# Carrying four row groups of the last expert into the first two tiles of each half, and writing the right half's products between the left half's tiles

## The chip, the cores and the metric

The kernel runs on one core of a Trainium2 chip. The core has a matrix engine (PE, also called TensorE) with a weight-load path of its own (PEld), a vector engine (DVE), a scalar engine (ACT), a general engine (POOL), which here issues the input loads, and SP, which here issues the stores. Sixteen DMA engines move the data for all queues. The metric is the device time of one execution in microseconds (us). The span in the profile runs from the first to the last instruction of one profiled execution, and is a little shorter than the time of that execution.

## What is computed

Attention with keys and values averaged over blocks of 8, for 8 batches and 8 heads of 576 x 64, and then a soft mixture of experts over the 4608 tokens of 512 columns:

```python
def _moe_ref(x, phi, w1, w2):            # x: 4608 x 512, 8 experts of 4 slots, F = 1024
    logits = x @ phi
    d = np.exp(logits - logits.max(0, keepdims=True))
    d /= d.sum(0, keepdims=True) + 1e-09
    slot_input = (d.T @ x).reshape(E, S_per_e, D)
    for e in range(E):
        h = np.maximum(slot_input[e] @ w1[e], 0.0)
        slot_out[e] = h @ w2[e]
    c = np.exp(logits - logits.max(1, keepdims=True))
    c /= c.sum(1, keepdims=True) + 1e-09
    return c @ slot_out.reshape(n_slots, D)
```

The output is 4608 x 512 in float32, 9.4 MB. The change lies in the last part: `h @ w2` for the last expert, and `c @ slot_out`.

## The kernel before

The attention runs over four pairs of batches and leaves, for each token, the exponentials of its logits, transposed into `cT` (128 partitions: four copies of the 32 slots; token columns). After the last pair come the two layers of the experts.

The first layer gives `h_sb`, which `turn_hidden` transposes into `hT` (128 rows of F within a group, 8 groups `fj`, 32 slot columns). `second_layer` (line 478) multiplies, for an expert and each of its 8 row groups `fj`, the 32 columns of `hT` by 128 rows of w2. The product has 32 rows only, so group `fj` writes the strip `fj % 4` of the accumulator `so_ps` in PSUM; the four strips are four partial sums that the final product adds, because `cT` holds its 32 slots four times. I call these products narrow (32 columns of weights) and the others full (128 columns).

w2 of the first seven experts arrives whole. The last expert's w2 comes as two halves of 256 columns, left and right, each in three pieces: row groups 0 to 3, 4 to 6, and 7 (`PIECES`, line 431; loads issued by POOL on line 435). PE works on it in an order written out by hand, as ACT, DVE and SP do from line 445 on.

For each half, `side` (line 551) does the following once groups 0 to 6 are in `so_ps`:

- ACT scales `so_ps` by `recC` into `so_a` (so far without group 7).
- Tiles 0 and 1 of the tokens are "carried": `product(n, cols, True)` adds, in a PSUM bank of its own, `zT[:, n]` times group 7 of w2 (line 537) and the tile's tokens times `so_a` (line 538). `zT` holds the tokens of the two tiles times the last expert's `h` of group 7, made ahead of time: line 498 puts that part of `h_sb`, scaled, into `hz` (otherwise zeros), line 501 multiplies it by `cT`, line 503 copies it out of PSUM.
- Between the two carried tiles, `second_layer` adds group 7 to `so_ps` itself, and DVE scales the whole into `so`.
- Tiles 2 to 7 are plain products of tokens and `so` (line 540).
- Each tile's product is scaled by `recR` on its way from PSUM to SBUF (`put`, line 543), on ACT (line 513) or DVE (line 515), and `store` (line 529) sends one or two tiles from SP.

The left half is finished before the right half begins. Tiles 0 to 7 are therefore stored in eleven small stores of 128 or 256 KB. After both halves, tiles 8 to 35 are made in full width of 512 columns, put by ACT and DVE in turn, and stored in four large stores (groups of 4, 6, 10 and 8 tiles). The products share five PSUM banks (`ps_f`). `busy` (line 507) writes products that are not used, while PE would wait for w2.

Of the kernel before, what the change touches and what calls it, by code (L numbers as in the profile page):

```python
# [8 lines left out]
FP = mybir.dt.float32  # L9
BF = mybir.dt.bfloat16  # L10
AF = mybir.ActivationFunctionType
ALU = mybir.AluOpType
# [6 lines left out]
def kernel(  # L19
# [10 lines left out]
    nc = tc.nc  # L30
# [4 lines left out]
    DM = H * D  # L35
    E = moe_w1.shape[0]
    F = moe_w1.shape[2]
    NS = moe_phi.shape[1]
# [10 lines left out]
    FJ = F // 128  # L49
    XW = D + NS  # L50
    HQ = H // 2
    NG = 128 // NS
# [7 lines left out]
    TILES = [(g, r) for g, (rows, _) in enumerate(GROUPS) for r in range(rows)]  # L60

    ctx.enter_context(tc.manual_schedule(engines={ET.Pool}))
    consts = ctx.enter_context(tc.tile_pool(name="consts", bufs=1))
# [10 lines left out]
    cT = persist.tile([128, 2, B * S // 2], BF)  # L74
# [80 lines left out]
    with tc.tile_pool(name="tmp", bufs=1) as tmp:  # L155
# [8 lines left out]
        for r in range(2):  # L164
            rows = slice(r * D, (r + 1) * D)
            nc.vector.tensor_copy(out=iphi[rows, :, 0:D],
                                  in_=ident[rows, rows].rearrange("p d -> p () d").to_broadcast([D, H, D]))
        spread = tmp.tile([128, J, H, NS], BF, name="spread")
        for j in range(J):
            nc.vector.tensor_tensor(out=spread[:, j],  # L170
                                    in0=phi_f[:, j].rearrange("p s -> p () s").to_broadcast([128, H, NS]),
                                    in1=head.rearrange("p h -> p h ()").to_broadcast([128, H, NS]), op=ALU.mult)
        phi_ps = ps_m.tile([128, H, NS], FP, name="phi_ps", tag="m")
        for j in range(J):
            nc.tensor.matmul(out=phi_ps, lhsT=sel[:, j].rearrange("p r a j -> p (r a j)"), rhs=spread[:, j],  # L175
                             start=(j == 0), stop=(j == J - 1))
        nc.scalar.copy(out=iphi[:, :, D:XW], in_=phi_ps)
    nc.vector.memset(siT, 0.0)
    hz = consts.tile([128, 128], BF)
    nc.vector.memset(hz, 0.0)  # L180

    att = ExitStack()
# [177 lines left out]
    def tokens(n):  # L360

        g, r = TILES[n]
        rows, base = GROUPS[g]
        step, c0 = rows // 2, base // 2 + r // 2
        return cT[:, r % 2, c0:c0 + 127 * step + 1:step]
# [64 lines left out]
    halves = [slice(0, HC), slice(HC, DM)]  # L430
    PIECES = ((0, 4), (4, FJ - 1), (FJ - 1, FJ))
    w2_half = [xsa[:, 1, i * FJ * HC:(i + 1) * FJ * HC].rearrange("p (j c) -> p j c", c=HC) for i in range(2)]
# [13 lines left out]
    post = ctx.enter_context(tc.tile_pool(name="post", bufs=1))  # L446
    ps_o = ctx.enter_context(tc.tile_pool(name="ps_o", bufs=1, space=PSUM))
    ps_f = ctx.enter_context(tc.tile_pool(name="ps_f", bufs=5, space=PSUM))

    recC = post.tile([128, 1], FP)  # L450
    h_sb = [post.tile([128, F], BF, name=f"h_sb{i}") for i in range(E // NG)]
# [24 lines left out]
    so_ps = ps_o.tile([128, DM], FP, name="so_ps")  # L476

    def second_layer(e, j0=0, j1=FJ, half=None):
        cols = slice(0, DM) if half is None else halves[half]
        for fj in range(j0, j1):  # L480
            g = fj % NG
            nc.tensor.matmul(out=so_ps[g * NS:(g + 1) * NS, cols], lhsT=hT[:, e, fj],  # L482
                             rhs=w2_at[e, fj] if half is None else w2_half[half][:, fj],
                             start=(e == 0 and fj < NG), stop=(e == E - 1 and fj >= NG), skip_group_check=True)
# [8 lines left out]

    J7 = FJ - 1
    P7 = (E - 1) % NG * NS
    nc.vector.tensor_scalar(out=hz[P7:P7 + NS], in0=h_sb[(E - 1) // NG][P7:P7 + NS, J7:F:FJ], scalar1=recC[P7:P7 + NS],
                            scalar2=None, op0=ALU.mult)
    z_ps = ps_f.tile([128, 2, 128], FP, name="z_ps", tag="f")  # L500
    nc.tensor.matmul(out=z_ps, lhsT=hz, rhs=cT[:, :, 0:128], start=True, stop=True)
    zT = post.tile([128, 2, 128], BF)
    nc.scalar.copy(out=zT, in_=z_ps)

    idle = ps_m.tile([128, 512], FP, name="idle_ps", tag="m")

    def busy(n):
        for _ in range(n):
            nc.tensor.matmul(out=idle, lhsT=ident, rhs=cT[:, 0, 0:512], start=True, stop=True)

    def scaled(engine, dst, src, by):
        if engine == 0:
            nc.scalar.activation(out=dst, in_=src, func=AF.Copy, scale=by)  # L513
        else:
            nc.vector.tensor_scalar(out=dst, in0=src, scalar1=by, scalar2=None, op0=ALU.mult)  # L515

    so_a = post.tile([128, DM], BF)
    so = post.tile([128, DM], BF)
# [3 lines left out]
    n = 0  # L522
# [6 lines left out]
    def store(g, r0, r1, cols):  # L529
        home, dst = places[g]  # L530
        nc.sync.dma_start(out=dst[:, r0:r1, cols], in_=home[:, r0:r1, cols])

    def product(n, cols, carried=False):
        ps = ps_f.tile([128, DM], FP, name="f_ps", tag="f")[:, 0:cols.stop - cols.start]
        if carried:
            half = halves.index(cols)
            nc.tensor.matmul(out=ps, lhsT=zT[:, n], rhs=w2_half[half][:, J7], start=True, stop=False)
            nc.tensor.matmul(out=ps, lhsT=tokens(n), rhs=so_a[:, cols], start=False, stop=True)
        else:
            nc.tensor.matmul(out=ps, lhsT=tokens(n), rhs=so[:, cols], start=True, stop=True)  # L540
        return ps

    def put(n, cols, engine, ps):
        g, r = TILES[n]
        scaled(engine, places[g][0][:, r, cols], ps, recR[:, n:n + 1])


    PARTS_L = ((0, 0, 1), (0, 1, 2), (1, 0, 1), (1, 1, 2), (2, 0, 2), (2, 2, 4))
    PARTS_R = ((0, 0, 1), (0, 1, 2), (1, 0, 2), (2, 0, 2), (2, 2, 4))

    def side(half, parts):
        cols = halves[half]
        scaled(0, so_a[:, cols], so_ps[:, cols], recC)
        ends = {(g, r1 - 1): (r0, r1) for g, r0, r1 in parts}
        f0 = product(0, cols, True)
        second_layer(E - 1, J7, FJ, half)
        f1 = product(1, cols, True)
        scaled(1, so[:, cols], so_ps[:, cols], recC)
        for n in range(8):
            ps = (f0, f1)[n] if n < 2 else product(n, cols)  # L560
            put(n, cols, 0 if n < 2 else 1 - n % 2, ps)
            if TILES[n] in ends:
                store(TILES[n][0], *ends[TILES[n]], cols)

    for e in range(E - 2):
        second_layer(e)
    busy(6)
    second_layer(E - 2)
    busy(3)
    for half, parts in enumerate((PARTS_L, PARTS_R)):  # L570
        for j0, j1 in PIECES[:-1]:
            second_layer(E - 1, j0, j1, half)
        side(half, parts)
    for n in range(8, len(TILES)):
        g, r = TILES[n]
        put(n, slice(0, DM), n % 2, product(n, slice(0, DM)))
# [32 lines left out]
```

## Time and profile before

| | |
|---|---|
| median of three runs | 176.9 us (176.53 to 177.4) |
| the profiled execution's own time | 177.83 us |
| its span | 175.9 us |
| mean granted PE clock | 0.846 |
| PE, ACT, DVE busy in the span | 132.1, 83.1, 90.9 us |
| instructions | 3088 |
| bytes written by SP's queue | 10.49 MB |

Rows of the timeline have the start in us from the span's start, the time taken, the engine, the line of the kernel, the operation, the tile written, the tiles read, the shape and how many instructions are merged; in brackets stands the idle time ahead of it and what ended that. "PE L482 MATMUL so_ps<-xsa,hT 128*32 128x256" is a narrow product: 128 x 32 weights, 256 columns streamed. `xsa` is the memory that the last expert's w2 is loaded into, `exa` and `w_sb` hold output tiles. Rows that begin with a stretch "a:b" give, after its length, the busy time of the engines in it. The end of a matmul is modelled.

### The profile page before, as it was taken

To read this page: it belongs to the slowest core of one execution; us is meant where nothing else is said; L and a number is where in the kernel's file an instruction comes from. 1 tells how busy PE (TensorE), PEld (TensorE's weight loads), DVE (VectorE), ACT (ScalarE), POOL (GpSimd) and SP (SyncE) were. 2 spreads that over 40 slices of the span, in tenths; PEclk is the share of its full clock that TensorE was granted. 3 is DMA by queue.
4 is the path that set the end of the run, shared out by engine and by line. 5 is a ranking of instruction groups with operands and counts; after the bars stand their busy time and mean duration, and the time that the engine had idled before them with its cause. 6 is when DMAs were issued, how large, how long until landed. Compare 5 with 4: busy or idle time off the path is not lost.

```text
span 175.9 us, 3088 instructions
## 1 busy us (share of the span) xinstructions
PE 132.1 (75%) x1239; PEld 77.9 (44%) x1240; DVE 90.9 (52%) x250; ACT 83.1 (47%) x154; POOL 18.8 (11%) x36
## 2 busy tenths in 40 slices
PE   5504889999999999799997987989970376998000
PEld 2202555766676667566664545444440122333000
DVE  4403242487777879768798498505340003589300
ACT  3200248876768369665699650630200004799000
POOL 7000111132110050100100020051010000000000
PEclk9955899999999999999999995555798589579855
DMA  5999999999999999999999999999999999789995
GB/s 199 232 218 216 220 216 213 220 210 221 209 209 203 212 219 214 218 216 214 216 211 222 216 214 212 224 214 214 212 220 218 214 189 169 260 328 432 464 387 238
DMA packets 8973, 41.14 MB, mean 234 GB/s; under 512 B 752, under 2 KB 4848, under 8 KB 4992
## 3 DMA queue, kind: packets, MB, share of 16 engines
q0 software_dynamic: 6016, 30.48, 84.7%
q1 hardware_dynamic: 2944, 10.49, 15.0%
q8 instruction: 9, 0.15, 0.3%
q14 instruction: 4, 0.03, 0.0%
HBM read 61.93 MB, written 9.44 MB: 406 GB/s over the span
## 4 chain that ended last, share of the span: by engine, by line
DMA 38%; PE 31%; issue 10%; DVE 6%; ACT 6%; POOL 2%; DVEq 0%; POOLq 0%; ACTq 0%
DMA xsa<-in_moe_w_dram 18%; DMA big<-in_q_dram 14%; DMA phi_f<-in_moe_phi_dram 7%; PE pool_ps L224 5%; PE sc L283 5%; PE u_ps L297 4%; PE f_ps L540 4%; PE q_ps L252 4%; ACT exa L285 3%; PE G_ps L319 2%; DVE w_sb L515 2%; PE lg_ps L315 2%; DVE xsa L308 1%; PE turn_ps L237 1%; ACT qTa L256 1%
## 5 line engine op out<-in xcount | busy, mean ns | idle before, releaser
L285 ACT ACTIVATE exa<-sc 72x576 bf16<-72x576 f32 x64 | 39.1, 649 | 11.8 <-PE sc L283 11.4
L308 DVE TENSOR_TENSOR xsa<-u_ps,rec 128x384 bf16<-128x384 f32 x69 | 37.6, 552 | 1.5
L297 PE MATMUL u_ps<-vp,exa 72*128 72x97 bf16 (+1 forms) x320 | 27.0, 221 | 1.5 <-DVE xsa L308 1.4
L283 PE MATMUL sc<-qTa,kp 64*72 64x288 bf16 x128 | 23.2, 304 | 1.8 <-ACT exa L285 1.7
L297 PEld LDWEIGHTS <-exa 72*128 72x128 bf16 (+1 forms) x320 | 17.6, 106 | 10.7 <-DVE xsa L308 3.7
L302 DVE RECIPROCAL rec<-u_ps 128x4 f32<-128x4 f32 x72 | 12.5, 177 | 14.6 <-PE u_ps L297 14.0
L224 PE MATMUL pool_ps<-big,pmat 128*128 128x320 bf16 (+1 forms) x128 | 19.9, 300 | 0.1
L224 PEld LDWEIGHTS <-pmat 128*128 128x128 bf16 x128 | 12.2, 102 | 4.4 <-issue 0.4
L252 PE MATMUL q_ps<-ident,big 128*128 128x128 bf16 x144 | 11.7, 219 | 2.3 <-DMA big<-in_q_dram 1.2
L540 PE MATMUL f_ps<-so,cT 128*128 128x512 bf16 (+1 forms) x40 | 11.3, 408 | 1.3 <-ACT w_sb L513 0.6
L283 PEld LDWEIGHTS <-kp 64*72 64x72 bf16 x128 | 8.5, 107 | 6.7 <-issue 2.3
L319 PE MATMUL G_ps<-xsa,ee 128*128 128x512 bf16 x36 | 10.7, 441 | 0.8 <-ACT ee L316 0.7
L515 DVE TENSOR_SCALAR so<-so_ps,recC 128x256 bf16<-128x256 f32 x2 | 1.0, 484 | 19.9 <-PE so_ps L482 19.9
L252 PEld LDWEIGHTS <-big 128*128 128x128 bf16 x144 | 8.6, 97 | 5.2 <-issue 1.8
L258 DVE COPY qTa<-q_ps 128x768 bf16<-128x768 bf16 x16 | 8.9, 555 | 3.8 <-PE q_ps L252 3.6
L515 DVE TENSOR_SCALAR w_sb<-f_ps,recR 128x512 f32<-128x512 f32 x14 | 9.5, 745 | 0.8 <-PE f_ps L540 0.6
L256 ACT COPY qTa<-q_ps 128x768 bf16<-128x768 bf16 x8 | 6.3, 793 | 6.3 <-PE q_ps L252 6.3
L513 ACT ACTIVATE w_sb<-f_ps,recR 128x512 f32<-128x512 f32 x14 | 8.7, 684 | 0.5 <-PE f_ps L540 0.3
L513 ACT ACTIVATE so_a<-so_ps,recC 128x256 bf16<-128x256 f32 x2 | 0.9, 473 | 16.5 <-PE so_ps L482 16.4
L482 PEld LDWEIGHTS <-hT 128*32 128x32 bf16 x72 | 2.1, 103 | 13.8 <-issue 12.9
L540 PEld LDWEIGHTS <-cT 128*128 128x128 bf16 x40 | 4.9, 122 | 7.0 <-issue 5.3
L175 PE MATMUL phi_ps<-spread,sel 128*128 128x256 bf16 x4 | 1.4, 383 | 8.6 <-DVE spread L170 8.6
(91 smaller groups left out, 157.2 us busy)
## 6 DMA issues: line engine op xcount, KB each, us to landing
w_sb<-in_moe_w_dram POOLq DMA_DIRECT2D x3, 2048.0 KB, 37.7
big<-in_q_dram POOLq DMA_DIRECT2D x4, 1152.0 KB, 13.2
big<-in_v_dram POOLq DMA_DIRECT2D x4, 1152.0 KB, 17.2
big<-in_moe_w_dram POOLq DMA_DIRECT2D x2, 2048.0 KB, 45.5
big<-in_k_dram POOLq DMA_DIRECT2D x3, 1152.0 KB, 21.9
out_dram<-w_sb SPq DMA_DIRECT2D x1, 2560.0 KB, 8.3
qTa<-in_moe_w_dram POOLq DMA_DIRECT2D x1, 2048.0 KB, 35.1
out_dram<-w_sb SPq DMA_DIRECT2D x1, 2048.0 KB, 10.5
```

The costliest lines, as they stand in the source:

```text
L224: nc.tensor.matmul(out=ps, lhsT=pmat, rhs=src[:, r0 * POOL + t:r1 * POOL:POOL, :], start=(t == 0), stop=(t == POOL - 1))
L252: nc.tensor.transpose(out=ps[:, t].rearrange("p n i -> p (n i)"), in_=q_sb[pair][:, tt:tt + 2, :].rearrange("p t d -> p (t d)"), identity= ...
L258: nc.vector.tensor_copy(out=dst, in_=ps)
L283: nc.tensor.matmul(out=ps[:, r, 0:S // 2], lhsT=kp[pair][rows, n], rhs=qT[pair][rows, n].rearrange("p t i -> p (t i)"), start=True, stop=True)
L285: nc.scalar.activation(out=dst.rearrange("p r (i t) -> p r i t", t=NU), in_=ps[:, :, 0:S // 2].rearrange("p r (t i) -> p r i t", i=NI), fu ...
L297: nc.tensor.matmul(out=ps[rows, hh], lhsT=ex[b][:, hh].rearrange("p r t -> p (r t)")[:, c:c + rows.stop - rows.start], rhs=vp[(2 * pair + ...
L302: nc.vector.reciprocal(out=rec, in_=ps[:, :, XW])
L308: nc.vector.tensor_tensor(out=dst, in0=ps[:, :, 0:XW], in1=rec.rearrange("p h -> p h ()").to_broadcast([128, HQ, XW]), op=ALU.mult)
L319: nc.tensor.matmul(out=ps, lhsT=ee[:, t].rearrange("p g s -> p (g s)"), rhs=x[:, t, :, 0:D], start=(t == 0), stop=(t == 8))
L513: nc.scalar.activation(out=dst, in_=src, func=AF.Copy, scale=by)
L515: nc.vector.tensor_scalar(out=dst, in0=src, scalar1=by, scalar2=None, op0=ALU.mult)
L540: nc.tensor.matmul(out=ps, lhsT=tokens(n), rhs=so[:, cols], start=True, stop=True)
```

## The change

`hz`, `zT` and the carry take four row groups (`HZ` = 4, groups 4 to 7) in place of group 7 alone. `so_a` is scaled when groups 0 to 3 are in (`first_rows`). The two carried tiles take first their product with `so_a` (`begin`), then four carries each, so that `so_ps` and the carried tiles use w2's pieces as they come (`begin` for the second piece, `finish` for the third). The right half's work is no longer behind the left half's: its `first_rows` stands between left tiles 3 and 4, its `begin` between left tiles 5 and 6, its `finish` behind left tile 7. Left tile 7 is put by DVE in place of ACT. The stores are the same eleven, in the same order.

```diff
-    hz = consts.tile([128, 128], BF)
+    HZ = F // 128 // 2
+    hz = consts.tile([128, HZ, 128], BF)
...
-    J7 = FJ - 1
+    J4 = FJ - HZ
     P7 = (E - 1) % NG * NS
-    nc.vector.tensor_scalar(out=hz[P7:P7 + NS], in0=h_sb[(E - 1) // NG][P7:P7 + NS, J7:F:FJ], scalar1=recC[P7:P7 + NS],
-                            scalar2=None, op0=ALU.mult)
-    z_ps = ps_f.tile([128, 2, 128], FP, name="z_ps", tag="f")
-    nc.tensor.matmul(out=z_ps, lhsT=hz, rhs=cT[:, :, 0:128], start=True, stop=True)
-    zT = post.tile([128, 2, 128], BF)
-    nc.scalar.copy(out=zT, in_=z_ps)
+    nc.vector.tensor_scalar(out=hz[P7:P7 + NS],
+                            in0=h_sb[(E - 1) // NG][P7:P7 + NS].rearrange("p (q j) -> p j q", j=FJ)[:, J4:FJ],
+                            scalar1=recC[P7:P7 + NS], scalar2=None, op0=ALU.mult)
+    zT = post.tile([128, HZ, 2, 128], BF)
+    for j in range(0, HZ, 2):
+        z_ps = ps_f.tile([128, 2, 2, 128], FP, name="z_ps", tag="f")
+        for i in range(2):
+            nc.tensor.matmul(out=z_ps[:, i], lhsT=hz[:, j + i], rhs=cT[:, :, 0:128], start=True, stop=True)
+        nc.scalar.copy(out=zT[:, j:j + 2], in_=z_ps)
...
+    def carry(ps, n, half, j0, j1):
+        for fj in range(j0, j1):
+            nc.tensor.matmul(out=ps, lhsT=zT[:, fj - J4, n], rhs=w2_half[half][:, fj], start=False, stop=(fj == FJ - 1))
...
-    def side(half, parts):
+    def first_rows(half):
+        second_layer(E - 1, 0, J4, half)
+        scaled(0, so_a[:, halves[half]], so_ps[:, halves[half]], recC)
+
+    def begin(half):
         cols = halves[half]
-        scaled(0, so_a[:, cols], so_ps[:, cols], recC)
-        ends = {(g, r1 - 1): (r0, r1) for g, r0, r1 in parts}
-        f0 = product(0, cols, True)
-        second_layer(E - 1, J7, FJ, half)
-        f1 = product(1, cols, True)
+        fs = [bank(cols) for n in range(2)]
+        for n, ps in enumerate(fs):
+            nc.tensor.matmul(out=ps, lhsT=tokens(n), rhs=so_a[:, cols], start=True, stop=False)
+        carry(fs[0], 0, half, J4, FJ - 1)
+        second_layer(E - 1, J4, FJ - 1, half)
+        return fs
+
+    def finish(half, fs):
+        cols = halves[half]
+        carry(fs[0], 0, half, FJ - 1, FJ)
+        second_layer(E - 1, FJ - 1, FJ, half)
+        carry(fs[1], 1, half, J4, FJ)
+        put(0, cols, 0, fs[0])
+        store(0, 0, 1, cols)
         scaled(1, so[:, cols], so_ps[:, cols], recC)
-        for n in range(8):
-            ps = (f0, f1)[n] if n < 2 else product(n, cols)
-            put(n, cols, 0 if n < 2 else 1 - n % 2, ps)
-            if TILES[n] in ends:
-                store(TILES[n][0], *ends[TILES[n]], cols)
+        put(1, cols, 0, fs[1])
+        store(0, 1, 2, cols)
...
-    for half, parts in enumerate((PARTS_L, PARTS_R)):
-        for j0, j1 in PIECES[:-1]:
-            second_layer(E - 1, j0, j1, half)
-        side(half, parts)
+    left, right = halves
+    first_rows(0)
+    fs = begin(0)
+    finish(0, fs)
+    put(2, left, 1, product(2, left))
+    store(1, 0, 1, left)
+    put(3, left, 0, product(3, left))
+    store(1, 1, 2, left)
+    first_rows(1)
+    put(4, left, 1, product(4, left))
+    put(5, left, 0, product(5, left))
+    store(2, 0, 2, left)
+    fs = begin(1)
+    put(6, left, 1, product(6, left))
+    put(7, left, 1, product(7, left))
+    store(2, 2, 4, left)
+    finish(1, fs)
+    for n in range(2, 8):
+        put(n, right, 1 - n % 2, product(n, right))
+        g, r = TILES[n]
+        if r % 2:
+            store(g, r - 1, r + 1, right)
     for n in range(8, len(TILES)):
```

More of the change, by code (lines that the diff above doesn't have):

```diff
@@ L531, in store, with bank, product @@
         nc.sync.dma_start(out=dst[:, r0:r1, cols], in_=home[:, r0:r1, cols])
[L533 to L540, printed above, removed]
-        return ps
+    def bank(cols):
+        return ps_f.tile([128, DM], FP, name="f_ps", tag="f")[:, 0:cols.stop - cols.start]
+    def product(n, cols):
+        ps = bank(cols)
+        nc.tensor.matmul(out=ps, lhsT=tokens(n), rhs=so[:, cols], start=True, stop=True)
+        return ps
+    def carry(ps, n, half, j0, j1):
+        for fj in range(j0, j1):
+            nc.tensor.matmul(out=ps, lhsT=zT[:, fj - J4, n], rhs=w2_half[half][:, fj], start=False, stop=(fj == FJ - 1))
     def put(n, cols, engine, ps):
@@ L545, in put @@
         scaled(engine, places[g][0][:, r, cols], ps, recR[:, n:n + 1])
-    PARTS_L = ((0, 0, 1), (0, 1, 2), (1, 0, 1), (1, 1, 2), (2, 0, 2), (2, 2, 4))
-    PARTS_R = ((0, 0, 1), (0, 1, 2), (1, 0, 2), (2, 0, 2), (2, 2, 4))
-    def side(half, parts):
+    def first_rows(half):
+        second_layer(E - 1, 0, J4, half)
+        scaled(0, so_a[:, halves[half]], so_ps[:, halves[half]], recC)
+    def begin(half):
         cols = halves[half]
-        scaled(0, so_a[:, cols], so_ps[:, cols], recC)
-        ends = {(g, r1 - 1): (r0, r1) for g, r0, r1 in parts}
-        f0 = product(0, cols, True)
-        second_layer(E - 1, J7, FJ, half)
-        f1 = product(1, cols, True)
-        scaled(1, so[:, cols], so_ps[:, cols], recC)
-        for n in range(8):
-            ps = (f0, f1)[n] if n < 2 else product(n, cols)
-            put(n, cols, 0 if n < 2 else 1 - n % 2, ps)
-            if TILES[n] in ends:
-                store(TILES[n][0], *ends[TILES[n]], cols)
+        fs = [bank(cols) for n in range(2)]
[11 more added lines that the diff above has]
+        store(0, 0, 1, cols)
+        scaled(1, so[:, cols], so_ps[:, cols], recC)
+        put(1, cols, 0, fs[1])
+        store(0, 1, 2, cols)
     for e in range(E - 2):
```

## The prediction

> **What bounds the kernel now.** I read the end of the span first: busy time, clock and DMA by stretches, then the SP queue's store issues.
>
> ```profile
> 153.00:154.50 1.50, 1.50 (x6) 0.59 (x4) 0.92 (x3) 1.50 (x4) 0.00 (x0) 0.50 0.31 107
> 154.50:157.00 2.50, 2.37 (x9) 0.91 (x7) 2.29 (x4) 2.17 (x5) 0.00 (x0) 0.72 1.01 351
> 157.00:174.00 17.00, 5.41 (x18) 1.96 (x17) 7.04 (x11) 5.94 (x10) 0.00 (x0) 0.77 1.01 425
> 148.00 0.34 SPq L531 DMA_DIRECT2D out_dram<-exa  x1
> 150.55 0.44 SPq L531 DMA_DIRECT2D out_dram<-exa  x1
> 151.57 0.34 SPq L531 DMA_DIRECT2D out_dram<-exa  x1
> 154.49 0.44 SPq L531 DMA_DIRECT2D out_dram<-exa  x1
> 156.01 0.34 SPq L531 DMA_DIRECT2D out_dram<-w_sb  x1
> ```
>
> The columns are stretch, length, busy time of PE, PE's weight loads, DVE, ACT and POOL, then granted clock, DMA share and GB/s. From 157 to 174 the DMA engines are full (1.01) and move 17 x 425 GB/s = 7.2 MB. That is the four large stores: 28 tiles of 128x512 f32 are 7.3 MB. So the end lies 18 us behind the first large store (156.01), wherever that store goes, so long as the small stores ahead of it are through. Those eleven small stores run from 148.00 to 154.49. Their transfers keep the engines full from 154.5 to 157, but between 153.0 and 154.5 only 0.31 busy: 0.69 x 1.5 = 1.0 us of DMA lost, waiting for the right side (its first store is issued at 151.57, 1.0 us behind the last of the left at 150.55). A change in the two halves is therefore worth what it moves (a) the first large store and (b) this hole.
>
> Ahead of that stands the load of w2, whose pieces PE waits for. These rows are the left half, in order:
>
> ```profile
> 145.33 0.29 PE L482 MATMUL so_ps<-xsa,hT 128*32 128x256 bf16 x4
> 146.34 0.29 PE L482 MATMUL so_ps<-xsa,hT 128*32 128x256 bf16 x3 [0.72 <-DMA xsa<-in_moe_w_dram]
> 146.67 0.47 ACT L513 ACTIVATE so_a<-so_ps,recC 128x256 bf16<-128x256 f32 x1 [16.44 <-PE so_ps L482]
> 146.80 0.27 PE L537 MATMUL f_ps<-xsa,zT 128*128 128x256 bf16 x1 [0.17 <-DMA xsa<-in_moe_w_dram]
> 147.20 0.27 PE L538 MATMUL f_ps<-so_a,cT 128*128 128x256 bf16 x1
> 147.40 0.28 PE L482 MATMUL so_ps<-xsa,hT 128*32 128x256 bf16 x1
> 147.51 0.47 ACT L513 ACTIVATE exa<-f_ps,recR 128x256 f32<-128x256 f32 x1 [0.36 <-PE f_ps L538]
> 147.61 0.28 PE L537 MATMUL f_ps<-xsa,zT 128*128 128x256 bf16 x1
> 147.73 0.27 PE L538 MATMUL f_ps<-so_a,cT 128*128 128x256 bf16 x1
> 147.79 0.48 DVE L515 TENSOR_SCALAR so<-so_ps,recC 128x256 bf16<-128x256 f32 x1 [18.31 <-PE so_ps L482]
> 148.33 0.27 PE L540 MATMUL f_ps<-so,cT 128*128 128x256 bf16 x1 [0.32 <-DVE so L515]
> ```
>
> The reader sees three things. The second piece lands at 146.3 and the third by 146.8. so_a stands between the second piece and the first put (146.67 to 147.14, then L538 at 147.20). And the gaps from start to start at full clock are 0.12 from one full product to the next (147.61 to 147.73), 0.20 from a full product to a narrow one (32 columns of weights, 147.20 to 147.40) and 0.21 back. A batch of up to four narrow ones goes abreast (four in 0.29).
>
> The right half runs at half clock:
>
> ```profile
> 149.04 0.87 DVE L515 TENSOR_SCALAR exa<-f_ps,recR 128x256 f32<-128x256 f32 x2
> 149.48 0.40 PE L482 MATMUL so_ps<-xsa,hT 128*32 128x256 bf16 x4
> 150.14 0.47 ACT L513 ACTIVATE so_a<-so_ps,recC 128x256 bf16<-128x256 f32 x1
> 150.97 0.39 PE L482 MATMUL so_ps<-xsa,hT 128*32 128x256 bf16 x1
> 151.29 0.39 PE L537 MATMUL f_ps<-xsa,zT 128*128 128x256 bf16 x1
> 151.47 0.48 DVE L515 TENSOR_SCALAR so<-so_ps,recC 128x256 bf16<-128x256 f32 x1 [1.56 <-PE so_ps L482]
> 152.01 0.59 PE L540 MATMUL f_ps<-so,cT 128*128 128x256 bf16 x2
> 153.24 1.06 PE L540 MATMUL f_ps<-so,cT 128*128 128x512 bf16 x2
> 153.67 1.06 PE L540 MATMUL f_ps<-so,cT 128*128 128x512 bf16 x2
> 142.22:145.64 3.42, 2.45 (x19) 0.77 (x18) 0.00 (x0) 0.00 (x0) 0.00 (x0) 1.00 1.33 185
> 145.64:149.05 3.41, 2.07 (x13) 1.01 (x13) 0.90 (x3) 1.72 (x4) 0.00 (x0) 1.00 1.10 157
> 149.05:152.46 3.41, 2.93 (x16) 0.97 (x16) 1.38 (x5) 2.43 (x6) 0.00 (x0) 0.50 0.84 283
> 152.46:155.88 3.42, 3.42 (x12) 1.48 (x11) 2.73 (x5) 2.92 (x6) 0.00 (x0) 0.50 0.68 230
> 155.88:159.29 3.41, 3.28 (x13) 1.33 (x12) 3.31 (x6) 3.41 (x7) 0.00 (x0) 1.00 0.99 392
> ```
>
> A 512-column product takes 0.43 (153.24 to 153.67), so a 256-column one 0.21; narrow to full takes 0.32 (150.97 to 151.29), full to narrow I take as 0.30, the 0.20 of the left stretched in the same measure. The granted clock falls at 149.05 and comes back at 155.88: exactly the stretch that the change rewrites.
>
> **The change, part by part.** *Four row groups in hz and z.* The memset is four times as long (at most 0.5 us, start of the kernel). The scaling into hz grows from 128 to 512 strided elements, four products of z replace one, two casts of 512 replace one of 256. These rows bound them:
>
> ```profile
> 2.94 0.11 DVE L180 MEMSET hz<- 128x64 uint32 x1
> 5.82 0.69 DVE L147 CAST big<-exa 128x1024 bf16<-128x1024 f32 x1 [2.76 <-DMA exa<-in_k_dram]
> 129.16 0.33 DVE L498 TENSOR_SCALAR hz<-h_sb,recC 32x128 bf16<-32x128 bf16 x1
> 129.86 0.37 ACT L503 CAST zT<-z_ps 128x256 bf16<-128x256 f32 x1 [2.66 <-PE z_ps L501]
> 139.14 1.90 PE L482 MATMUL so_ps<-qTa,hT 128*32 128x512 bf16 x16 [7.47 <-DMA qTa<-in_moe_w_dram]
> ```
>
> Below, hz costs nothing more; above, 4 x 0.33, so +1.0 us, with 0.4 for three z products. PE then still idles 6 of its 7.47 us for w2, DVE's next work is at 147.79 and ACT's at 146.67. The memset ends before DVE's 2.76 us of idle time. All of this costs 0; without that cover it would be 1.5 us. POOL's loads keep their order and nothing is moved past them.
>
> *Left half.* so_a needs four groups only: 145.62 + 0.04, so 145.66 to 146.13. The two products of so_a follow at 146.19 and 146.31, and three carries at 146.42 to 146.65 (the second piece landed at 146.3). Three narrow ones at 146.85, the last carry of tile 0 at 147.06, a narrow one at 147.26, the four carries of tile 1 from 147.47 to 147.82. Put 0 can start at 147.06 + 0.27 + 0.04 = 147.37 in place of 147.51; so at 147.26 + 0.39 = 147.65 in place of 147.79 (0.39 is the distance of the rows 147.40 and 147.79); the first plain product at 148.19 in place of 148.33. So the one microsecond by which so_a is earlier comes down to 0.14 us of gain, because six more products (per side 2 + 8 in place of 4) and one more change between narrow and full stand in the queue.
>
> *Right half.* The four narrow products follow tile 3 (148.30 + 0.20 = 148.50) and so_a comes behind puts 1 and 3 on ACT, at 149.0 to 149.5, 1.1 us earlier than 150.14. The clock falls at 149.05 as now, and PE's queue is then, from 149.55: two products, three carries (last starts 150.39), three narrow ones 150.69, tile 6 at 151.01, tile 7 at 151.22, a carry 151.43, a narrow one 151.73, four carries from 152.05 to 152.68, the first plain right product at 152.89. It now starts at 152.01. That is +0.88. Of this, tiles 6 and 7 of the left also hang on it: they now go ahead of the right half, and will be put by DVE one after the other (151.44, then 0.42 later by the row of two puts in 0.87) and end at 152.34. Their store is SP's, and SP holds the first right store behind it: 152.4 in place of 150.55, and right tile 0 at about 152.9 in place of 151.57. DVE's so of the right waits behind these two puts, till 152.3, and ends at 152.8, just before PE is free for the product. PSUM has five banks and none is late here: tile 2's, which the second right product takes, is free by 149.
>
> *The sum.* The first large store moves with the plain products: +0.88, and 0.05 for the SP's three last small stores, which press together: +0.93. The hole in DMA does not close it: the small store of tiles 4 and 5 is issued at about 150.1 as now; with a DMA pause till the next at 152.4 it grows from 1.0 to some 1.5 us, so the small stores are through 0.5 to 1.0 us later, and the large ones start behind them. I take +0.9. Against the profiled execution's own 177.83 us (span 175.9) that is 178.7; that execution lies 0.9 above the median of the runs shown, 176.9, on whose scale the forecast is **177.8 us**. Bounds: +0.4 where the clock is the same in both but full for part of the right half, +1.5 where the fall comes one half window sooner and the left half's eight carries are slowed as well (eight times 0.1, and two changes between narrow and full at 0.1).
>
> [...]
>
> **The rivals.** *The denser PE keeps its clock (faster).* In the stretch 145.64 to 149.05 before has nine full 256-column products and four narrow ones; after has fourteen and eight.
>
> ```profile
> 129.76 1.91 PE L482 MATMUL so_ps<-big,hT 128*32 128x512 bf16 x32
> 101.26:104.68 3.42, 2.84 (x35) 1.61 (x33) 3.07 (x11) 2.33 (x4) 0.71 (x2) 1.00 1.04 218
> ```
>
> For it: the clock outlived the stretch with these 32 narrow products, which go four abreast, so 8 x 512 = 4096 columns; after has 14 x 256 + 2 x 256 = 4096 too. Against it: it fell behind the stretch from 101.26 with 2.84 us of busy PE. Busy time does not decide, and the columns are about even. With full clock the right half takes 4 x 0.12 + 0.20 + 0.21 + 0.24 + 0.20 + 0.21 + 0.36 = 1.9 us from 149.55; the plain products would then start at 152.1 (DVE's so behind tiles 6 and 7), not earlier than now, but the next tiles go at DVE's pace and not PE's 0.43: the first large store is 0.8 us earlier. The small stores, held on SP, give back half of it: -0.35, **176.5**, at most -0.8 or 176.1.
>
> *The clock is the same in both and mostly full (little changes).* [...] At full clock before's plain right product would be bound by ACT and DVE at about 151.7, after's at 152.1: +0.4, **177.3**. The spread of the runs shown, 176.53 to 177.4, allows for it.
>
> *The early so_a pays in full.* If the carries, whose operands are at hand early, slip into PE's waits, right tile 0 could follow so_a's lead of 1.1 us, and the 1.0 us hole in DMA would be filled: -1.0, **175.9**. Against it: PE's order is written out, and tiles 6 and 7 and two narrow batches stand before that carry.
>
> **How the numbers follow.** Forecast (right half longer at half clock, +0.9) 0.50; clock kept 0.25; same full clock 0.15; lead in full 0.10. A measurement of this kernel tells about 0.5%, 0.9 us, from no change. Of the forecast's 0.50, 0.38 lies above that bound; of the kept clock 0.12 below it and 0.13 within; of the same clock 0.05 above, 0.10 within; the last all below. Slower 0.43, same 0.35, faster 0.22. The range, 176.1 to 178.6, leaves out the lead in full and the ends of the others; the forecast's own range is 177.3 to 178.4.
>
> **What would show it.** Right: so_a of the left at about 145.7, the first put only 0.1 to 0.2 earlier; granted clock 0.5 from about 149; the store of left tiles 6 and 7 issued two microseconds later relative to that of tiles 4 and 5; the first large store at about 156.9; DMA full behind it for 17 us. Wrong: a granted clock near 1.0 between 149 and 156, a first large store before 155.5, or a small-store phase without a hole.

## The result, and the profile after

| | before | changed |
|---|---|---|
| median of six runs | 177.31 us (176.53 to 178.01) | 179.27 us (178.88 to 180.12) |
| the profiled execution | 177.83 us, span 175.9 | 178.99 us, span 177.2 |
| PE clock, mean granted | 0.846 | 0.871 |

The changed kernel is slower: ratio 1.0121, 95% interval 1.0083 to 1.0158, so 2.1 us (1.5 to 2.8). The forecast was 177.8 us on a median of 176.9, 0.9 us slower.

These are the stretches that were read before, the first of them also for the kernel before. The columns are as there; the last three are granted clock, DMA share and GB/s. A transfer is counted in the stretch in which it begins, so a share can exceed 1. Before, then after:

```profile
149.00:156.00 7.00, 6.50 (x27) 2.51 (x26) 4.23 (x9) 5.51 (x12) 0.00 (x0) 0.51 0.76 258
```

```profile
149.00:156.00 7.00, 6.02 (x34) 2.87 (x34) 5.33 (x11) 5.32 (x12) 0.00 (x0) 1.00 0.77 260
151.50:153.00 1.50, 1.10 (x7) 0.70 (x8) 1.12 (x4) 1.19 (x4) 0.00 (x0) 1.00 0.50 173
153.00:154.50 1.50, 1.50 (x7) 0.61 (x6) 1.35 (x3) 1.50 (x5) 0.00 (x0) 1.00 0.79 264
154.50:157.00 2.50, 2.30 (x9) 0.88 (x8) 2.50 (x5) 2.50 (x6) 0.00 (x0) 1.00 1.05 372
```

Two things stand out. The clock is full from 149 to 156, where it was 0.51 before. And the hole in DMA has moved from 153.0 to 154.5 to 151.5 to 153.0 (share 0.50), where the store of left tiles 6 and 7 is late. SP's rows show it: the first store, those of left tiles 4 and 5 and of 6 and 7, and the first large store. The row of before for tiles 4 and 5 stands first:

```profile
150.06 0.39 SPq L531 DMA_DIRECT2D out_dram<-exa  x1
```

```profile
147.62 0.34 SPq L535 DMA_DIRECT2D out_dram<-exa  x1
149.78 0.40 SPq L535 DMA_DIRECT2D out_dram<-exa  x1
151.34 0.38 SPq L535 DMA_DIRECT2D out_dram<-exa  x1
155.29 0.34 SPq L535 DMA_DIRECT2D out_dram<-w_sb  x1
```

The store of tiles 6 and 7 comes 1.56 us behind that of 4 and 5 (before: 150.55 - 150.06 = 0.49). Still, the first large store is issued at 155.29, 0.72 us earlier than in the profile of before. By the prediction's reading the end should be earlier too. The end in short stretches:

```profile
172.00:173.00 1.00, 0.00 (x0) 0.00 (x0) 0.00 (x0) 0.00 (x0) 0.00 (x0) 0.50 0.65 279
173.00:173.50 0.50, 0.00 (x0) 0.00 (x0) 0.00 (x0) 0.00 (x0) 0.00 (x0) 0.50 1.23 524
173.50:174.00 0.50, 0.00 (x0) 0.00 (x0) 0.00 (x0) 0.00 (x0) 0.00 (x0) 0.50 0.09 33
174.00:175.00 1.00, 0.00 (x0) 0.00 (x0) 0.00 (x0) 0.00 (x0) 0.00 (x0) 0.50 0.08 33
175.00:177.20 2.20, 0.00 (x0) 0.00 (x0) 0.00 (x0) 0.00 (x0) 0.00 (x0) 0.50 0.00 0
```

From 173.0 to 173.5 sixteen transfers of 16 KB begin (524 GB/s), from then on one at a time: 33 GB/s and a share of 0.08 are one engine of sixteen. By the transfers in the trace, fifteen engines end between 173.6 and 174.0, some 0.3 to 0.5 us earlier than in before (all sixteen between 174.1 and 174.3), and then one works on alone until 175.5. In before only sixteen transfers of 4 bytes begin from 174 to 175:

```profile
174.00:175.00 1.00, 0.00 (x0) 0.00 (x0) 0.00 (x0) 0.00 (x0) 0.00 (x0) 0.50 0.01 0
```

What did this one do in the meantime? The queues of the DMA view, whole span, first before, then after:

```profile
q8 instruction: 9, 0.15, 0.3%
out_dram<-w_sb SPq DMA_DIRECT2D x1, 2048.0 KB, 10.5
```

```profile
q8 instruction: 10, 0.16, 0.4%
out_dram<-w_sb SPq DMA_DIRECT2D x1, 2048.0 KB, 13.0
```

And the same view of after from 156 to 160:

```profile
q1 hardware_dynamic: 356, 1.72, 106.1%
q8 instruction: 1, 0.02, 2.3%
```

There is a tenth transfer of instructions on queue q8, 16 KB, among the large stores. Its 2.3% of 16 engines over 4 us are 1.47 us of one engine, about as long as one engine works on alone; the last store lands 13.0 us behind its issue in place of 10.5. I call such a transfer a refill. Refills go with PE's instructions: in before the first comes at 29.4 us with 228 PE records behind it (products and weight loads), the ninth at 131.3 with 2282, so one in 257 on average (single steps are some 210 to 300). The counts shortly ahead of the tenth in after (first), and at the end of before; each count is the sum of the first two x-numbers:

```profile
0.00:156.50 156.50, 127.12 (x1240) 76.91 (x1241) 85.41 (x242) 77.63 (x146) 18.81 (x36) 0.89 1.02 217
```

```profile
0.00:175.90 175.90, 132.11 (x1239) 77.86 (x1240) 90.94 (x250) 83.06 (x154) 18.81 (x36) 0.85 1.00 234
```

The tenth came after 2481 records; before has 2479 in all. So before's program seems to end just short of it, and the change adds 30 PE instructions: 15 products (three for z, six a half), each with its weight load.

### The profile page after: what moved, and what is told of

It reads as the page before. It is cut to its first block, busy times and chain, and to the rows that moved or that the text cites. A ratio compares the mean times of both kernels' runs of the same rounds, so it can differ in the third digit from the quotient of the medians.

```text
span 177.2 us, 3118 instructions
## 1 busy us (share of the span) xinstructions
PE 131.8 (74%) x1255; PEld 78.5 (44%) x1255; DVE 91.7 (52%) x251; ACT 82.8 (47%) x154; POOL 18.8 (11%) x36
## 4 chain that ended last, share of the span: by engine, by line
DMA 42%; PE 30%; issue 7%; ACT 5%; DVE 4%; POOL 2%; DVEq 0%; POOLq 0%; ACTq 0%
DMA xsa<-in_moe_w_dram 22%; DMA big<-in_q_dram 14%; DMA phi_f<-in_moe_phi_dram 7%; PE pool_ps L225 5%; PE sc L284 4%; PE u_ps L298 4%; PE q_ps L253 4%; PE f_ps L542 3%; ACT exa L286 3%; PE G_ps L320 2%; DVE w_sb L519 2%; PE lg_ps L316 1%; PE turn_ps L238 1%; ACT qTa L257 1%; PE so_ps L483 1%
## 5 line engine op out<-in xcount | busy, mean ns | idle before, releaser
L542 PE MATMUL f_ps<-so,cT 128*128 128x512 bf16 (+1 forms) x40 | 10.2, 346 | 1.4 <-ACT w_sb L517 0.8
L276 ACT CAST vp<-v_ps 72x384 bf16<-72x384 f32 x16 | 7.0, 483 | 0.0
```

## The experiments

The theory to test, **refill theory**: most of the loss is the tenth refill on one DMA engine among the large stores. The rivals: **order theory**, the loss is the right half's place between the left tiles (tiles 6 and 7 late, the hole at 151.5); and **carry theory**, it is the six further products of each half. Ratios are to before on the same chip, five rounds each; the medians of before in the three groups were 177.24, 176.9 and 177.02 us. A ratio is not the quotient of the two medians (they differ by up to 0.25%); conclusions go by the ratios and their 95% intervals.

### Instructions taken away, added, and moved

Changed kernel with fewer unused products at the start (PE waits for the loads there):

```diff
-    warm(8, warm_ps)
+    warm(1, warm_ps)
...
-            warm(6, junk)
+            warm(0, junk)
```

> The changed kernel with 13 of the 14 unused products of the start left out (26 PE instructions fewer, 4 more than before in place of 30; PE idles there for the loads). Refill theory (the change's 30 further PE instructions bring a tenth 16 KB refill of the q8 queue, at 156.5 us, onto one of the 16 DMA engines among the large stores, 1.47 us of it): the tenth refill is gone, no single engine works on alone behind 173.5, and the time is 0 to 0.8 us under before. Order theory (tiles 6 and 7 behind the right half's products, the hole in the stores at 151.5): nothing of it is touched, so 1.5 to 2.5 us over before as the changed kernel is.

Measured: 177.8 us, ratio 1.0030 (1.0000 to 1.0061). The tenth refill is gone, and the last engine ends 0.13 us behind the others. Order theory's 1.5 to 2.5 us are not there; refill theory's 0 to 0.8 us under before are not reached either, so something smaller is left.

Before with products added that are not used, in the stretch where PE waits for the fifth expert's w2:

```diff
+    def tiny(n):
+        for _ in range(n):
+            nc.tensor.matmul(out=idle[:, 0:1], lhsT=ident, rhs=cT[:, 0, 0:1], start=True, stop=True)
+
     for e in range(E - 2):
         second_layer(e)
+        if e == 3:
+            tiny(15)
     busy(6)
```

> Before with 15 unused products of one column added while PE waits for the fifth expert's w2 (30 PE instructions, as many as the change adds; about 1 us of an idle stretch of 7.5 us). Refill theory: a tenth q8 refill at 155 to 160 us, one DMA engine alone at the end, 1.0 to 2.2 us slower than before. Order theory: nothing happens, within 0.4 us of before.

Measured: 178.47 us, ratio 1.0084 (1.0057 to 1.0111): 1.5 us for 15 products in idle time. The queue in the stretch from 157 to 158 (5.8% of 16 us are 0.93 us of one engine), and the end:

```profile
q8 instruction: 1, 0.02, 5.8%
```

```profile
172.00:173.00 1.00, 0.00 (x0) 0.00 (x0) 0.00 (x0) 0.00 (x0) 0.00 (x0) 0.50 1.19 508
173.00:174.00 1.00, 0.00 (x0) 0.00 (x0) 0.00 (x0) 0.00 (x0) 0.00 (x0) 0.50 0.12 49
174.00:175.00 1.00, 0.00 (x0) 0.00 (x0) 0.00 (x0) 0.00 (x0) 0.00 (x0) 0.50 0.08 33
```

The same picture as in after, without any of the change: a refill among the large stores, and then one engine of sixteen on its own.

Before with the start's 13 products left out (the edit of the first kernel), as a control:

> Before with 13 of the 14 unused products of the start left out: the control for the start. Both theories: within 0.5 us of before, nine q8 refills. If it is over 0.8 us faster or slower, the start counts and the first kernel says nothing of the refill.

Measured: 177.33 us, ratio 1.0007 (0.9983 to 1.0030), with nine refills. The start counts for nothing that can be told here.

The changed kernel with those 13 left out and `tiny(13)` in their place later:

> The changed kernel with the 13 products of the start left out and 13 unused products of one column added while PE waits for w2: the same number of PE instructions as the changed kernel. Refill theory: the tenth refill is back at about 156.5 us and the time is 1.5 to 2.5 us over before, as the changed kernel; 1.5 us or more over the changed kernel with fewer. Order theory: the same as the changed kernel with fewer.

Measured: 179.18 us, ratio 1.0108 (1.0071 to 1.0145). The tenth refill is back (156 to 157), and with it 1.4 us (179.18 - 177.8; 1.5 or more were expected). So it is the number of instructions, not what they are.

### The refill moved in time

Before with `tiny(60)`:

> Before with 60 unused products of one column (120 PE instructions) in the same idle stretch, 3 to 4 of its 7.5 us: the tenth refill comes some 45 products sooner, at 149 to 152 us among the small stores, where DMA has holes. If the refill costs by the large stores that queue behind it on its one engine: 0 to 0.6 us over before, since that engine catches up in the holes. If it costs the same wherever it comes among the stores: 1.0 to 1.6 us over before, as with 15.

Measured: 177.04 us, ratio 0.9997 (0.9971 to 1.0023). The refill now comes at 147.7, when the last of w2 is arriving and the first small store is issued, and not at 149 to 152 as expected, so a refill among the small stores stays untested:

```profile
q8 instruction: 1, 0.02, 8.5%
```

These 8.5% of 16 us are 1.36 us of one engine, about as much as in after. But here, 7 us ahead of the large stores, they cost nothing that can be measured; DMA has holes behind them (share 0.13 from 149 to 150). Then the same on the changed kernel, nothing left out, `tiny(45)` added; and the changed kernel itself beside it:

> The changed kernel with 45 unused products of one column added while PE waits for w2 (90 PE instructions more; some 2.5 us of a 6.8 us idle stretch), nothing left out. If the tenth refill costs because it comes among the large stores (refill theory as the last four runs left it), it now comes 45 products sooner, near 147 us, before the stores, no engine works on alone at the end, and adding work makes the kernel faster: 1.000 to 1.006 of before, as with fewer instructions, and 0.8 to 2.0 us under the changed kernel of the same call. If the refill costs wherever it comes, or the length of PE's program does: 1.010 to 1.016, as the changed kernel or slower.

> The changed kernel itself, for comparison on the same chip as the kernel with 45 products added. All theories: 1.008 to 1.016 of before.

Measured: 177.8 us, ratio 1.0053 (1.0032 to 1.0074), and for the changed kernel 179.22 us, 1.0122 (1.0100 to 1.0144). Ninety more instructions make the changed kernel 1.4 us faster by the medians, 0.7% by the ratios. No engine works on alone for long at the end (0.19 us):

```profile
172.00:173.00 1.00, 0.00 (x0) 0.00 (x0) 0.00 (x0) 0.00 (x0) 0.00 (x0) 0.50 0.88 377
173.00:174.00 1.00, 0.00 (x0) 0.00 (x0) 0.00 (x0) 0.00 (x0) 0.00 (x0) 0.50 0.39 164
174.00:175.00 1.00, 0.00 (x0) 0.00 (x0) 0.00 (x0) 0.00 (x0) 0.00 (x0) 0.50 0.00 0
```

The single transfers in the traces show the same engine by engine. Sixteen transfers of 4 bytes go with each large store, one at the end of each engine's share. The table has the times of the fifteenth and the sixteenth:

| | refill at | first large store: fifteenth, sixteenth | last large store: fifteenth, sixteenth |
|---|---|---|---|
| before | none late | 159.53, 159.62 | 174.27, 174.27 |
| changed | 156.7 | 159.40, 160.94 | 173.98, 175.53 |
| before, 15 products added | 157.8 | 159.32, 160.69 | 173.91, 175.28 |
| before, 60 added | 147.7 | 158.85, 159.16 | 173.57, 173.75 |
| changed, 13 left out | none late | 159.38, 159.65 | 174.10, 174.23 |
| changed, 45 added | 147.5 | 159.02, 159.36 | 173.75, 173.94 |

Where the refill is late, one engine is 1.54 or 1.37 us behind the others from the first large store on and never catches up. In before with 15 products added it is the one that carried the refill: each of its transfers in the first large store begins 3 to 4 ns before the one ahead of it ends. Traced back so, with no second candidate at any step, they lead to one that begins 14 ns before the refill ends. Refill and lag are not the same length: there the refill took 0.93 us, and the first transfer behind it 0.72 in place of 0.31.

### What is left: order or carries

All four that follow have the 13 products of the start left out, so nine refills. Their peers are before with fewer (1.0007) and the changed kernel with fewer (1.0030). The right half wholly behind the left:

```diff
-    first_rows(1)
     put(4, left, 1, product(4, left))
     put(5, left, 0, product(5, left))
     store(2, 0, 2, left)
-    fs = begin(1)
     put(6, left, 1, product(6, left))
-    put(7, left, 1, product(7, left))
+    put(7, left, 0, product(7, left))
     store(2, 2, 4, left)
+    first_rows(1)
+    fs = begin(1)
     finish(1, fs)
```

> The changed kernel without its tenth refill (13 products of the start left out), and with the right half written wholly behind left tile 7, which ACT puts again: four groups carried, nothing between the left tiles. That the right half stands between the left tiles costs (tiles 6 and 7 and their store held up): this is 0.3 to 0.6 us faster than the changed kernel with fewer (ratio 1.003 to before), so 0.999 to 1.001. That the eight carries of the right half cost (six more products ahead of the first plain one): 0 to 0.3 us slower than it, 1.003 to 1.005, with the first store of the right 0.3 to 0.8 us later from the first store than in before with fewer.

Measured: 177.79 us, ratio 1.0025 (0.9999 to 1.0050). The hole is behind that store now: DMA share 0.81 from 151.5 to 153, 0.41 from 153 to 154.5. The first right store comes 4.04 us behind the first store (before with fewer 3.17), a little more than carry theory had; the ratio lies between the two expectations.

Only tiles 6 and 7 ahead of the right half's carries:

```diff
-    fs = begin(1)
     put(6, left, 1, product(6, left))
-    put(7, left, 1, product(7, left))
+    put(7, left, 0, product(7, left))
     store(2, 2, 4, left)
+    fs = begin(1)
     finish(1, fs)
```

> The changed kernel without its tenth refill, and with left tiles 6 and 7 and their store ahead of the right half's carries (tile 7 put by ACT); the right half's first rows stay between tiles 3 and 4. Order theory for what is left of the loss: the store of tiles 6 and 7 comes 0.5 us behind that of 4 and 5 in place of 1.55, the hole in DMA from 151.5 to 153 (share 0.50) closes to over 0.8, and the time is 0.997 to 1.001 of before, 0.3 to 0.8 us under the changed kernel with fewer. Carry theory: the hole moves behind that store, and the time stays at 1.003.

Measured: 177.46 us, ratio 1.0017 (0.9980 to 1.0055). The hole closes as order theory had it. First the changed kernel with fewer, then this one:

```profile
151.50:153.00 1.50, 0.97 (x8) 0.56 (x7) 1.12 (x4) 0.96 (x3) 0.00 (x0) 1.00 0.50 171
```

```profile
151.50:153.00 1.50, 1.36 (x9) 0.67 (x8) 1.35 (x4) 1.47 (x5) 0.00 (x0) 1.00 0.94 328
```

But the time moved by less than the intervals. One row group carried (and with it one product of z in place of four), and the right half between the left tiles as the change has it:

```diff
-    HZ = F // 128 // 2
+    HZ = 1
...
```

> The changed kernel without its tenth refill, carrying one row group (as before) in place of four, with the right half between the left tiles as the change has it. Order theory: tiles 6 and 7 are still put late and one after the other by DVE, so the hole in the stores stays and the time is 1.002 to 1.005 of before. Carry theory: without the six further products per half it is at 0.999 to 1.001.

Measured: 177.38 us, ratio 1.0003 (0.9977 to 1.0029), as carry theory had it. And an attempt at something better than both kernels: one group, only the right half's first rows between tiles 5 and 6, tile 7 put by ACT:

> An attempt at a version better than both: one row group carried as before, the changed kernel's functions, 13 products of the start left out, and only the right half's first rows moved, to between left tiles 5 and 6 (tiles 6 and 7 ahead of the carry, tile 7 put by ACT). Order theory: so_a of the right comes up to 0.4 us sooner and nothing is held up, so the first right store comes 2.8 to 3.2 us behind the first store (3.17 in before with fewer) and the time is 0.996 to 1.000 of before. Rival: DMA is full by then anyway and the time is that of before, 0.999 to 1.002.

Measured: 176.83 us, ratio 0.9986 (0.9961 to 1.0012): not told from before.

Put in a square, one group gives 1.0007 with the halves apart and 1.0003 between the tiles, four groups 1.0025 and 1.0030. That leans to the carries and away from the place, but each interval is about as wide as the difference, so the times don't show it. The profiles, one execution each and all at full clock from 149 to 156, say more of where it comes from. This is how far the first large store is issued behind the first small one:

| kernel, 13 products left out | us | ratio |
|---|---|---|
| before | 6.69 | 1.0007 |
| changed | 7.65 | 1.0030 |
| changed, right half behind the left | 7.56 | 1.0025 |
| changed, tiles 6 and 7 ahead of the carries | 6.85 | 1.0017 |
| one group, right half between the tiles | 6.73 | 1.0003 |
| one group, only first rows between 5 and 6 | 6.54 | 0.9986 |

So with four groups this store comes 0.9 us later in two of the three orders, and 0.16 in the third; in these profiles it is neither the carries alone nor the place alone. That something is left in the time without the refill is shown by the kernel with 45 products added, 1.0053 (1.0032 to 1.0074); for the changed kernel with fewer, 1.0030, the interval begins at 1.0000.

## Why the prediction was wrong

**The way was right, the size was not**: forecast 0.9 us slower, measured 2.1. The step that failed is the pricing of the 30 added PE instructions. The prediction priced them by the time they run: under a wait for w2 ("All of this costs 0"), or as steps in PE's queue. Its sum has no term for fetching them. That term is 1.2 to 1.5 us: 0.7% between the changed kernel and the one with 45 products more, 0.8% from the products added to before. It shows where the prediction says "So the end lies 18 us behind the first large store (156.01), wherever that store goes": in after fifteen engines end 18.3 to 18.7 us behind that store, the sixteenth 20.2. With the refill out of the way the change costs 0.3% to 0.5%, 0.5 to 0.9 us. The upper bound is mis-added, too: its own terms, +0.9, eight times 0.1 and two times 0.1, add up to +1.9 and not +1.5, and that is still short of the 2.1 measured. Its "half window", a fall of the clock some 3.4 us sooner (half of the 6.83 from 149.05 to 155.88), no run shows: in after the clock was full from 141.9 to 165.8.

**The clock was a second miss.** The forecast carried "The granted clock falls at 149.05" over to the changed kernel. The clock there was 1.00, one of the signs of being wrong that the prediction names (another, a first large store before 155.5, came too: 155.29). When the clock falls differs between executions of one kernel: in the two profiles of the changed kernel it was 1.00 and 0.50 from 97 to 102 us. From 149 to 156 it was 0.51 in the profile of before and full in all twelve others, those of before with fewer or more instructions among them. Before itself was profiled once, so how often it has the full clock there is not shown. The first row is before with fewer, the second before with 15 products added:

```profile
149.00:156.00 7.00, 5.95 (x33) 2.51 (x33) 5.43 (x11) 6.35 (x14) 0.00 (x0) 1.00 0.89 307
```

```profile
149.00:156.00 7.00, 5.82 (x34) 2.43 (x32) 5.43 (x11) 6.35 (x14) 0.00 (x0) 1.00 0.85 288
```

So the denser PE did not earn the full clock, as the first rival had it: kernels with the halves of before have it too. What sets the clock no run shows. What applies is the rival of equal clocks, with a chance of 0.15 and +0.4 us by its working. At full clock in both, the first plain right product comes 5.79 us behind the first narrow ones in before with fewer (151.20 - 145.41) and 6.68 in the changed kernel with fewer (152.08 - 145.40): 0.9 later, with the last transfer of w2 over at 148.8 in both. The rival had 6.8 right for the changed kernel, and 6.4 (151.7 - 145.33) too late for before. That the forecast's +0.88 for this product is of the same size is luck: it was worked out with the right half at half clock in both. The way came out right in part by the same luck, and for the larger part because of the refill, which the prediction does not have.

**The left half was right to the hundredth, against the profile of before.** Rows of after:

```profile
145.08 0.29 PE L483 MATMUL so_ps<-xsa,hT 128*32 128x256 bf16 x4
145.42 0.47 ACT L517 ACTIVATE so_a<-so_ps,recC 128x256 bf16<-128x256 f32 x1 [14.25 <-PE so_ps L483]
147.12 0.47 ACT L517 ACTIVATE exa<-f_ps,recR 128x256 f32<-128x256 f32 x1 [1.23 <-PE f_ps L547]
147.41 0.48 DVE L519 TENSOR_SCALAR so<-so_ps,recC 128x256 bf16<-128x256 f32 x1 [17.80 <-PE so_ps L483]
147.95 0.38 PE L542 MATMUL f_ps<-so,cT 128*128 128x256 bf16 x2
```

From the first narrow products to put 0, to so and to the first plain product it takes 2.04, 2.33 and 2.87 us; worked out were 2.04, 2.32 and 2.86. Against before (2.18, 2.46, 3.00) that is the 0.14 us of gain. It hangs on when the second piece of w2 comes: in before PE used it 1.01 us behind the first narrow products, in before with fewer 0.63 us, and there so and the first plain product come after 2.09 and 2.62 us, against 2.34 and 2.87 in the changed kernel with fewer.

**The right half** ran by the first rival's working at full clock: it placed the first plain product at 152.1, 6.8 us behind the first narrow ones at 145.33.

```profile
150.11 0.28 PE L542 MATMUL f_ps<-so,cT 128*128 128x256 bf16 x1
150.43 0.48 DVE L519 TENSOR_SCALAR exa<-f_ps,recR 128x256 f32<-128x256 f32 x1 [1.15 <-PE f_ps L542]
151.23 0.48 DVE L519 TENSOR_SCALAR so<-so_ps,recC 128x256 bf16<-128x256 f32 x1
151.76 0.50 PE L542 MATMUL f_ps<-so,cT 128*128 128x256 bf16 x3 [0.39 <-DVE so L519]
```

It came 6.7 us behind them (151.76 - 145.08), and DVE's so stood behind the puts of tiles 6 and 7, as worked out. The store of these tiles was late, by 1.1 us and not by two, and the hole in DMA is there. (The five banks that the prediction counts are those of the pool `ps_f`.) In the profiled execution all this is 0.3 to 0.5 us to the good on fifteen engines, since before's own profile was the one at half clock, and the sixteenth turned it into a loss.

**The end.** "DMA full behind it for 17 us" was read as one resource. It is sixteen, and the kernel ends with the last of them.

## What to carry to other kernels

Count the instructions of an engine before adding some, even in idle time: here each further block of some 257 PE records was a transfer on one DMA engine, and where that fell among stores that keep all sixteen busy, the kernel ended with one engine, 1.3 to 1.6 us behind the others. Here 26 instructions fewer, or 90 more so that it came earlier, were worth more than the rest of the change; look for a stretch at the end with a DMA share near one sixteenth (here 0.08). And do not carry the granted clock of one profile over to another kernel: weigh a forecast at both clocks.

## What the runs showed of the hardware

- A refill of 16 KB took 0.9 to 1.8 us of one DMA engine. It cost the kernel 1.2 to 1.5 us when it came at 156 to 158 us, among 7.3 MB of stores, and nothing that could be measured at 147.5 to 147.7, ahead of the large stores.
- In all four profiles with a late refill one DMA engine was 1.3 to 1.6 us behind the fifteenth at the end of each of the four large stores, by the same amount each time; without a late refill the last engine was at most 0.6 us behind. In before with 15 products added, where its transfers can be followed back without a second candidate, it is the engine that carried the refill.
- Profiles with up to 2483 PE records (products and weight loads) have nine refills, those with 2509 or more ten. Where in between the tenth begins was not tried.
